# Sort-attention and gated MLP on one core: column sums of Sinkhorn by fp32 matmul, the first q as fp32, more transposes by DMA, the flag read in mid stream

## The chip, the cores and the metric

The kernel runs on one core of a Trainium2 chip. The metric is the device time of one execution in microseconds (us). The core has a matmul engine (TensorE, PE; its weight loads are listed apart as PEld), a vector engine (VectorE, DVE), an activation engine (ScalarE, ACT), GpSimd (POOL) and SyncE (SP). SP and POOL issue transfers to the DMA engines; SP's go by the hardware queue, POOL's by the software queue, which here also changes fp32 to bf16 on the way. Each engine takes its instructions in the order in which the program gives them.

## The reference

Inputs are fp32: q, k, v of shape (4, 8, 768, 64) (batch, head, sequence, head width), a sorting matrix of 8 x 8 for each batch and head, and the weights of a gated MLP. Cut to what matters:

```python
P = sort_net                                    # (4, 8, 8, 8)
for _ in range(5):
    P = P - np.max(P, axis=-1, keepdims=True)
    P = np.exp(P)
    P = P / (np.sum(P, axis=-1, keepdims=True) + 1e-09)
    P = P / (np.sum(P, axis=-2, keepdims=True) + 1e-09)
k_sorted = np.einsum('bhij,bhjcd->bhicd', P, k_b)   # 8 blocks of 96 rows are mixed
v_sorted = np.einsum('bhij,bhjcd->bhicd', P, v_b)
scores = scale * np.matmul(q_b, k_sb.transpose(0, 1, 2, 4, 3))  # inside a block, 96 x 96
attn = softmax(scores); x = attn @ v_sb             # (4, 768, 512) after merging heads
h = np.maximum(x @ w_in, 0.0); u, v = h[..., :512], h[..., 512:]
v_n = (v - mean(v)) / np.sqrt(var(v) + 1e-06)
v_s = np.einsum('ts,bsd->btd', w_spatial, v_n) + b_spatial[None, :, None]
out = (u * v_s) @ w_out                             # (4, 768, 512) fp32
```

## The kernel before

All of the work is cut into small units, functions named `u_XX`, and a text, `ORDER`, lists them in the order in which they are issued. An item such as `KT:2:D:0:2` calls `u_KT` with the arguments 2 (the PSUM tile), D (copied out by DVE; A is ACT), 0 (batch), 2 (pair of heads). The order in this text is the order on every engine: an engine that waits for one unit's data holds up all later units on it. There are four PSUM tiles, `ps0` to `ps3`, each used by one unit at a time.

The first part, for each batch: `L` loads q, k, v (POOL's queue, to bf16); `S0` loads the sorting matrices (SP's queue); `SK` is one Sinkhorn round, on 32 partitions (one for each batch and head) of 64 numbers: an exponential on ACT, then on DVE a row sum, a reciprocal, a product, a column sum, a reciprocal, a product. The maximum is left out; whether the sums stayed in range is looked at afterwards (`CK`, `CF`), and a flag is set for a slower general path if they did not. `PR` spreads the result over 128 partitions by matmuls, `P0` (DVE, batch 0) and `PD` (POOL, later batches) make of it block matrices `pd`, by which PE mixes k (`KT`, both mixed and turned) and v (`VT` and `VB` for batch 0; `VM` and eight SBUF-to-SBUF moves `VC` on SP's queue for the others). `QT` and `QQ` turn q on PE (one or two pairs of heads). `SC` makes the scores of four blocks and their exponential on ACT; `AT` multiplies by v and divides on DVE, giving `x_sb`. That has to be turned for the next product: `XT` does it on PE, with a copy from PSUM; `XD` does it by a DMA transpose on SP's queue.

The second part, for each batch: `VP` and `UP` are the two halves of the product with `w_in` (with relu on ACT or DVE), `ST`, `LN`, `LA` the normalization, `WT` the turning of `w_spatial` on PE (once), `SP` the spatial product and its bias on DVE, `GT` the gate, `OP` the product with `w_out`, `OE` its copy from PSUM and `OS` the transfer to the output. The second part of a batch is woven into the first part of the next. `OP` for the last batch is split: the first three of four inputs first, the fourth when it is ready. `o_sb` has two buffers, so a tile waits until the transfer of the tile two before it has landed.

`DM` are matmuls on zeros at the start, 36 in all, whose result is not used. `CK` (five checks on DVE), `CF` (a matmul that joins them, and two DVE steps that write the flag) and `LF` (every engine reads the flag into a register) stand at the end of `ORDER`; the branch follows. `BI` loads the bias over all partitions on SP's queue.

What sets the order around the change: POOL's queue holds, in this order, q, k and v of batch 0, v and k of batch 1, building `ident`, q of batch 1, then weights; SP's queue holds the sorting matrices, and nothing else until the first `VC`.

## Time and profile before

| | us |
|---|---|
| median of three runs (164.16 to 164.29) | 164.26 |
| the profiled execution: its own time | 163.99 |
| its span, from the first to the last instruction | 162.2 |
| PE, DVE, ACT, POOL busy | 147.9, 117.7, 84.3, 33.7 |
| mean granted clock of PE | 0.988 |

A page of the profile lists engines' busy times, groups of instructions by source line with the mean length of one, and the chain of work that ended last, followed back from the end. Lines such as `L569 PE MATMUL ps<-wspT,v_sb` name the source line, the engine, and what is written from what. The busy time in tenths over 40 slices of the span (about 4 us each) and the rates of the DMA engines:

```profile
PE   6988999899999979999999999999999999999700
DVE  4797899667897853748898888789787798267500
ACT  3144999858976476577654453557400155402420
DMA  2999999999999990479985996002059200243370
GB/s 12 191 204 205 203 205 205 210 220 237 271 206 204 206 172 0 69 133 148 184 188 94 225 149 195 0 36 97 0 107 237 113 0 0 91 172 129 129 250 25
```

The groups of instructions of the units in question, with busy time and mean length:

```profile
L307 PE MATMUL ps<-ident,q_in 128*64 128x128 bf16 x192 | 7.0, 220 | 1.1 <-DMA q_in<-in_q_dram 0.5 <-DVE kt L109 0.3 <-issue 0.3
L498 PE MATMUL ps<-ident,x_sb 96*128 96x96 bf16 x64 | 3.7, 206 | 0.0
L219 PE MATMUL ps<-warm 128*128 128x512 bf16 x35 | 9.9, 436 | 1.3 <-DVE warm L192 1.3
xT<-x_sb SPq DMA_TRANSPOSE x4, 5.1
```

(The last is from the list of transfers: four issued by SP, 5.1 us from issue to landing in the middle.)

### The profile page before, as it was taken

The numbers are of one execution on the slowest core, as the hardware profiler recorded it, in microseconds if no ns is written. First come the engines' busy times: TensorE is split into PE (matmuls) and PEld (weight loads), VectorE is DVE, ScalarE is ACT, GpSimd is POOL, SyncE is SP. The second block draws the span as 40 slices with busy tenths as digits, with TensorE's granted clock in tenths as the row PEclk, the third lists the DMA queues.
The fourth block names the chain that finished last, engine by engine and source line by source line (L and its number), as shares of the span: only waits on it lengthen the run. The fifth ranks groups of instructions, "written<-read, shape, count | busy, mean of one in ns | idle before, by whom it ended". The sixth has DMA issues, their size and how long they took to land.

```text
span 162.2 us, 3967 instructions
## 1 busy us (share of the span) xinstructions
PE 147.9 (91%) x1646; PEld 89.5 (55%) x1657; DVE 117.7 (73%) x265; ACT 84.3 (52%) x118; POOL 33.7 (21%) x39
## 2 busy tenths in 40 slices
PE   6988999899999979999999999999999999999700
PEld 2345777756677755455657656555666445655300
DVE  4797899667897853748898888789787798267500
ACT  3144999858976476577654453557400155402420
POOL 7946322470000434280000001600000000120000
PEclk9999999999999999999999999999999999999995
DMA  2999999999999990479985996002059200243370
GB/s 12 191 204 205 203 205 205 210 220 237 271 206 204 206 172 0 69 133 148 184 188 94 225 149 195 0 36 97 0 107 237 113 0 0 91 172 129 129 250 25
DMA packets 27351, 23.20 MB, mean 143 GB/s; under 512 B 7232, under 2 KB 24128, under 8 KB 27328
## 3 DMA queue, kind: packets, MB, share of 16 engines
q0 software_dynamic: 14864, 12.19, 48.5%
q1 hardware_dynamic: 12464, 10.70, 25.8%
q8 instruction: 14, 0.23, 0.5%
q14 instruction: 9, 0.07, 0.1%
HBM read 24.78 MB, written 6.29 MB: 192 GB/s over the span
## 4 chain that ended last, share of the span: by engine, by line
PE 78%; ACT 7%; DVE 6%; DMA 2%; issue 2%; DVEq 0%; ACTq 0%
PE ps L569 20%; PE ps L557 13%; PE ps L514 13%; PE ps L595 11%; PE ps L468 4%; PE ps L422 4%; PE ps L363 3%; PE ps L390 3%; PE ps L307 3%; ACT ex L427 2%; ACT kt L107 2%; PE ps L498 2%; DMA out_dram<-o_sb 1%; PE ps L504 1%; ACT o_sb L107 1%
## 5 line engine op out<-in xcount | busy, mean ns | idle before, releaser
L569 PE MATMUL ps<-wspT,v_sb 128*128 128x384 bf16 x192 | 33.2, 326 | 0.0
L427 ACT ACTIVATE ex<-ps 96x768 bf16<-96x768 f32 x32 | 24.4, 806 | 12.4 <-PE ps L422 12.3
L585 POOL TENSOR_TENSOR gt<-z,u_sb 128x768 bf16<-128x768 f32 x7 | 11.4, 1640 | 92.7 <-DVE z L575 42.1
L569 PEld LDWEIGHTS <-v_sb 128*128 128x128 bf16 x192 | 18.2, 98 | 11.9 <-issue 0.2
L575 DVE TENSOR_TENSOR z<-ps,b_bc 128x768 f32<-128x768 f32 x16 | 15.3, 957 | 11.6 <-PE ps L569 11.5
L557 PE MATMUL ps<-xT,w_in_sb 128*128 128x384 bf16 x128 | 23.3, 326 | 0.0
L476 DVE TENSOR_TENSOR x_sb<-ps,rec_all 96x512 bf16<-96x512 f32 x32 | 22.0, 687 | 1.1
L514 PE MATMUL ps<-w_in_sb,xT 128*128 128x512 bf16 x89 | 22.2, 379 | 0.4
L595 PE MATMUL ps<-w_out_sb,gt 128*128 128x512 bf16 x93 | 22.0, 379 | 0.2
L107 ACT COPY o_sb<-ps 128x1024 f32<-128x1024 f32 (+1 forms) x12 | 9.8, 835 | 14.8 <-PE ps L595 12.9
L531 DVE BATCH_NORM_STATS2 stats<-v_sb 128x6 f32<-128x512 bf16 x24 | 16.2, 677 | 1.0 <-ACT v_sb L113 0.9
L113 ACT ACTIVATE v_sb<-ps 128x1024 bf16<-128x1024 f32 (+1 forms) x8 | 7.4, 920 | 17.6 <-PE ps L514 17.6
L557 PEld LDWEIGHTS <-w_in_sb 128*128 128x128 bf16 x128 | 11.8, 98 | 7.6
L595 PEld LDWEIGHTS <-gt 128*128 128x128 bf16 x96 | 9.2, 98 | 10.2
L514 PEld LDWEIGHTS <-xT 128*128 128x128 bf16 x96 | 9.0, 98 | 9.6 <-DVE x_sb L476 0.2
L113 ACT ACTIVATE u_sb<-ps 128x768 bf16<-128x768 f32 x13 | 10.6, 812 | 5.1 <-PE ps L557 5.0
L107 ACT CAST kt<-ps 128x768 bf16<-128x768 f32 (+1 forms) x14 | 8.7, 641 | 7.9 <-PE ps L363 5.5
L468 PEld LDWEIGHTS <-ex 96*128 96x128 bf16 x256 | 10.5, 97 | 3.6 <-issue 0.3
L468 PE MATMUL ps<-vb,ex 96*128 96x65 bf16 x256 | 11.9, 193 | 0.1
L219 PE MATMUL ps<-warm 128*128 128x512 bf16 x35 | 9.9, 436 | 1.3 <-DVE warm L192 1.3
L422 PE MATMUL ps<-qT,kt 64*128 64x96 bf16 x256 | 9.5, 204 | 1.6 <-ACT kt L107 1.3
L422 PEld LDWEIGHTS <-kt 64*128 64x128 bf16 x256 | 6.2, 94 | 6.9 <-issue 3.8
(87 smaller groups left out, 179.0 us busy)
## 6 DMA issues: line engine op xcount, KB each, us to landing
out_dram<-o_sb SPq DMA_DIRECT2D x9, 512.0 KB, 4.3
q_in<-in_q_dram POOLq DMA_DIRECT2D x4, 768.0 KB, 18.0
k_in<-in_k_dram POOLq DMA_DIRECT2D x4, 768.0 KB, 15.1
v_in<-in_v_dram POOLq DMA_DIRECT2D x4, 768.0 KB, 21.5
vb<-vm SPq DMA_DIRECT2D x24, 99.0 KB, 3.1
out_dram<-o_sb SPq DMA_DIRECT2D x6, 256.0 KB, 3.2
ws_in<-in_moe_w_spatial_dram POOLq DMA_DIRECT2D x2, 576.0 KB, 26.4
w_in_sb<-in_moe_w_in_dram POOLq DMA_DIRECT2D x2, 512.0 KB, 26.0
```

Source lines behind the costliest of these rows:

```text
L107: nc.scalar.copy(out=out, in_=in_)
L113: nc.scalar.activation(out=out, in_=in_, func=AF.Relu)
L422: nc.tensor.matmul(t[:, hh, 0:HW].rearrange("p (g x) -> p g x", g=G)[:, :, ii * TB:(ii + 1) * TB], lhsT=kT[rows, i * BLK:i * BLK + 128], r ...
L427: nc.scalar.activation(out=e_tile(b, hp, ih).rearrange("p h (x g) -> p h x g", g=G), in_=t[0:BLK, :, 0:HW].rearrange("p h (g x) -> p h x g ...
L468: nc.tensor.matmul(t[:, hh, ii * VW:ii * VW + D + 1], lhsT=e[:, c:c + 128], rhs=vb[b % 2][:, ih * NI + ii, 2 * hp + hh, 0:D + 1], start=Tr ...
L476: nc.vector.tensor_mul(out=x_sb[:, hp].rearrange("p i (h d) -> p h i d", h=2), in0=tv[:, :, :, 0:D], in1=_raw_ap(rec, 0, [rec.ap[0], [NI, ...
L514: nc.tensor.matmul(t[:, x, :], lhsT=st["xT", b][:, n // 3, kc, (n % 3) * 128:(n % 3 + 1) * 128], rhs=w_in_sb[:, kc, DH:DFF], start=(kc == ...
L531: nc.vector.bn_stats(out=stats, in_=st["v_sb", b, n])
L557: nc.tensor.matmul(t[:, x, 0:HW], lhsT=w_in_sb[:, kc, mc * 128:(mc + 1) * 128], rhs=st["xT", b][:, ih, kc, :], start=(kc == 0), stop=(kc = ...
L569: nc.tensor.matmul(t[:, x, 0:HW], lhsT=st["v_sb", b, n][:, mc * 128:(mc + 1) * 128], rhs=wspT[:, 3 * x:3 * x + 3, n, :], start=(n == 0), s ...
L575: nc.vector.tensor_add(out=z.rearrange("p (x c) -> p x c", x=2), in0=t[:, :, 0:HW], in1=b_bc.rearrange("p (x c) -> p x c", x=2),)
L595: nc.tensor.matmul(t[:, x, :], lhsT=st["gt", b, mc][:, (n0 + x) * 128:(n0 + x + 1) * 128], rhs=w_out_sb[:, mc, :], start=(mc == 0), stop=( ...
```

## The change

Five things change together, and `ORDER` is written anew.

1. *Sinkhorn.* The sorting matrices lie as 2 halves of 128 rows (16 batch-and-head pairs of 8 rows each) of 8 numbers; a half is batches 0 and 1, or 2 and 3. `SX` does the exponential, with the row sum summed by the same ACT instruction, a reciprocal and a product by a per-row number on DVE. `SK` makes the column sums, already spread over the rows of their block, by one fp32 matmul with the matrix `same` (128 x 128, ones where two rows belong to one pair; built once by `SB` on DVE and POOL), then a reciprocal from PSUM and a product on DVE. In the first round ACT copies the column sums for the later check. In the last round the result is written as bf16 and spread 16 times along the row (`p_sp`); `PR` turns it by one matmul for each half. The mask is made by eight matmuls (`MK`) and not by a DVE sum.
2. *The first q.* `LH` loads q of batch 0 as fp32, in two halves, by SP's queue right after the sorting matrices; `QC` casts it to bf16, two pairs of heads on POOL and two on ACT. POOL's queue now first builds `ident` and `same`, and then loads k and v of batch 0 in halves, heads 4 to 7 before 0 to 3 for k. The mixing begins with heads 4 and 5.
3. *Transposes by DMA.* The output of batch 1's attention is turned by `XD` (it was `XT`). q of batch 3 is loaded early, put in order by four POOL copies (`QP`) and turned by one DMA transpose (`QX`); it was two `QQ`.
4. *The flag.* `CK` follows the last `AT` of batch 3, `CF` the next `OP`, and `LF` stands some ten units later, in the middle of the last batch's second part.
5. *Warm matmuls.* 10 `DM` matmuls in place of 36. A new unit `WX` is defined and not used.

The first and the last lines of the new `ORDER`, and the part with the turned output:

```diff
+ID BH S0:0 SB CO IV:2 S0:1 LH:0 SX:0:0 LH:1 L:k:0:4:8 SX:1:0 L:v:0:4:8 L:v:0:0:4 L:k:0:0:4 QC:P:0 L:v:1:0:8 L:k:1:0:8
+QC:P:3 IV:1 L:wv L:q:1:0:8 DM:0:4:512 SK:1:0:0 SX:0:1 MK:3 SK:3:1:0 IV:0 SK:0:0:1 SX:1:1 DM:0:1:512 L:wu SX:0:2
+DM:3:1:512 SK:2:1:1 QC:A:1 SK:3:0:2 SX:1:2 SX:0:3 QT:0:D:0:1 QC:A:2 DM:3:1:512 L:q:3:0:8 DM:2:1:512 SK:2:0:3 SK:3:1:2
+SX:0:4 QT:2:D:0:0 DM:1:2:512 SK:3:0:4 SX:1:3 L:wsa QT:3:A:0:3 PR:2:0 PC:A:0 P0:4:6 PD:1:0:4 P0:6:8 SK:1:1:3 SX:1:4
+VT:3:A:0:2 P0:2:4 PD:1:4:8 P0:0:2 QT:1:A:0:2 KT:0:A:0:2 SK:3:1:4 VB:2:D:0:2 VT:3:A:0:1 KT:1:D:0:3 SC:0:0:2:0
...
+AT:1:1:0:0 LA:0:5 SC:0:1:1:0 WT:3:A:0 LA:0:1 AT:1:1:3:0 AT:0:1:1:0 WT:2:A:4 XD:1:0 BI L:v:2:0:8 WT:3:D:2 LA:0:3
+SC:1:1:2:1 WT:0:D:3 WT:3:D:5 KT:1:D:2:1 KT:2:A:2:2 AT:0:1:2:1 KT:3:A:2:3 KT:2:A:2:0 AT:1:1:0:1 XD:1:1 SP:3:0:1
+VM:2:A:2:3 VM:1:D:2:0 L:q:2:0:8 SP:0:0:3 VM:2:D:2:2 VM:3:A:2:1 VC:2:0:4 GT:P:0:3 QQ:1:A:2:2 QQ:0:D:2:0 VC:2:4:8
+QX:3:0:4 VP:2:D:1:0:1 SC:1:2:3:1 SC:0:2:0:1 VP:3:A:1:4:5 SC:2:2:1:0 GT:D:0:1 ST:1:1 SC:1:2:2:1 L:v:3:0:8 ST:1:0 ST:1:4
...
+UP:2:A:3:1:1 GT:D:2:2 SP:1:3:0 SP:3:3:1 GT:P:3:0 SP:1:3:2 OP:3:2:4 GT:P:3:2 OS:1:4 OE:A:2:4 OS:1:0 OP:2:2:2 OP:1:2:0
+OE:A:2:0 GT:D:3:1 SP:0:3:3 GT:D:3:3 OS:2:4 OP:1:3:0:0:3 OS:2:0 OE:A:2:2 OP:0:3:2:0:3 OP:-1:3:0:3:4 OE:A:3:0:1:2
+OP:-1:3:2:3:4 OE:A:3:0:0:1 OP:2:3:4:0:3 OS:2:2 OE:A:3:2:1:2 OS:3:0:1:2 OP:-1:3:4:3:4 OE:A:3:2:0:1 OS:3:0:0:1
+OS:3:2:1:2 OS:3:2:0:1 OE:A:3:4:0:1 OE:A:3:4:1:2 OS:3:4:0:1 OS:3:4:1:2
```

The new functions, cut to the path taken:

```diff
+    def u_SB():
+        nc.vector.memset(same, 1.0)
+        for base, way in ((0, 1), (NB - 1, -1)):
+            nc.gpsimd.affine_select(
+                out=same, in_=same, compare_op=ALU.is_ge, fill=0.0, base=base,
+                pattern=[[-way * NB, 128 // NB], [0, NB]], channel_multiplier=way)
+    def u_SX(half, n, safe=False):
+        x, e, r = p_in[:, half], p_ex[:, half], p_row[:, half]
+        rows = (first_r if n == 0 else sums)[:, half]
...
+            nc.scalar.activation(out=e, in_=x, func=AF.Exp, accum_out=rows)
+        nc.vector.reciprocal(out=inv[:, half], in_=rows)
+        nc.vector.tensor_scalar(out=r, in0=e, scalar1=inv[:, half], scalar2=None, op0=ALU.mult)
+    def u_SK(ps, half, n, safe=False):
+        to = p16[:, half] if n == 4 else p_in[:, half]
+        t = ps_tile(ps)[:, 0, 0:NB]
+        nc.tensor.matmul(t, lhsT=same, rhs=r, start=True, stop=True)
...
+            if n == 0:
+                nc.scalar.copy(out=first_c[:, half], in_=t)
+            nc.vector.reciprocal(out=e, in_=t)
+        nc.vector.tensor_mul(out=to, in0=e, in1=r)
+        if n == 4:
+            nc.vector.tensor_copy(out=p_sp[:, half], in_=to.to_broadcast([128, NB, TB]))
+    def u_PR(ps, half):
+        t = ps_tile(ps)[:, 0, 0:128]
+        nc.tensor.matmul(t, lhsT=p_sp[:, half].rearrange("p j t -> p (j t)"), rhs=ident, start=True, stop=True)
+    def u_LH(half):
+        lo = int(half) * H // 2
+        st["q32", int(half)] = t = ld.tile([128, H // 2, G * D], FP32, name="q32", tag="ld")
+        nc.sync.dma_start(out=t, in_=_raw_ap(q, lo * S * D, [[G * D, 128], [S * D, H // 2], [1, G * D]]))
+    def u_QC(eng, hp):
+        to, of = st["q", 0][:, 2 * hp:2 * hp + 2], st["q32", hp // 2][:, 2 * (hp % 2):2 * (hp % 2) + 2]
+        if eng == "P":
+            nc.gpsimd.tensor_copy(out=to, in_=of)
+        else:
+            copy(eng, to, of)
```

`QP`, `QX` and `XD` are in the kernel before (`QP` and `QX` unused there).

More of the change, by code (lines that the diff above doesn't have):

```diff
@@ L650, in general_path @@
         st.clear()
[L651 to L656 removed]
+        for half in range(2):
+            u_S0(half)
+            for n in range(5):
+                u_SX(half, n, safe=True)
+                u_SK(0, half, n, safe=True)
+            u_PR(0, half)
+            if half == 0:
+                u_P0(0, 8)
+            u_PC("A", half)
         for b in range(B):
```

160 lines of the change are left out of this document (71 added, 89 removed).

## The prediction

> **What bounds the kernel now.** I read the page's engine totals first, then busy time by windows, then the chain of waits and the time line of the two ends, then the landing times of the transfers.
>
> ```profile
> span 162.2 us, 3967 instructions
> PE 147.9 (91%) x1646; PEld 89.5 (55%) x1657; DVE 117.7 (73%) x265; ACT 84.3 (52%) x118; POOL 33.7 (21%) x39
> PE 78%; ACT 7%; DVE 6%; DMA 2%; issue 2%; DVEq 0%; ACTq 0%
> ```
>
> The matmul engine sets the time, but not everywhere. The windows (length, then busy time of PE, PEld, DVE, ACT, POOL, granted clock, DMA share, GB/s) show two stretches where it is not full:
>
> ```profile
> 13.20:33.30 20.10, 18.27 (x415) 14.72 (x416) 16.28 (x32) 17.20 (x24) 7.93 (x10) 1.00 1.28 205
> 55.60:59.90 4.30, 3.43 (x90) 2.85 (x88) 2.44 (x4) 2.76 (x6) 1.64 (x1) 1.00 1.28 202
> ```
>
> From 13.2 to 33.3 us ACT and DVE, which empty PSUM, are busy 17.2 and 16.3 of 20.1 us: they pace the first batch's attention. The chain of waits through the second stretch (start, length, what) names the second batch's output, turned on PE (L498), and then the copies of `xT` and `kt`:
>
> ```profile
> 55.59 0.36 PE ps L498 x8
> 55.97 0.80 ACT xT L107
> 56.76 0.39 ACT kt L107
> 57.18 0.42 DVE kt L109
> 58.12 0.56 DVE kt L109
> 58.70 0.49 ACT kt L107
> 59.58 0.43 PE ps L390 x2
> ```
>
> At the start one Sinkhorn round is six steps one behind another. The last round's exponential starts at 9.43 us, the one before at 7.67, so a round takes 1.76:
>
> ```profile
> 9.43 0.26 ACT L231 ACTIVATE p_all<-p_all 32x64 f32<-32x64 f32 x1 [1.50 <-DVE p_all L242]
> 9.95 0.19 DVE L235 RECIPROCAL rowsum<-rowsum 32x8 f32<-32x8 f32 x1
> 10.18 0.21 DVE L236 TENSOR_TENSOR p_all<-p_all,rowsum 32x64 f32<-32x64 f32 x1
> 11.19 0.23 DVE L244 STREAM_TRANSPOSE p_t<-p 32x64 bf16<-32x64 bf16 x1
> ```
>
> At the end the last copy is done at 155.39 us, and SP then waits for the last output transfers to land; it passes the last of its landing waits at about 160.0. Its read of the flag lies under that wait:
>
> ```profile
> L639 SPq TENSOR_LOAD <-flag x1: 912/912/912, 156.2 to 156.2; - x1
> L696 SPq EVENT_SEMAPHORE  x8: 17/17/17, 157.7 to 160.0; - x8
> ```
>
> **The change, part by part.** The sum is made against the profiled execution: span 162.20, its time 163.99, so 1.79 us lie around the span; it is 0.27 below the median of 164.26, to which I add the difference.
>
> *Start, up to the first L514 matmul (32.84 us now).* Removed: five rounds on 32 rows of 64, `spread`, the stream transpose. Added: two interleaved halves of 128 rows of 8. Per round and half: exponential 0.26 (L231), reciprocal 0.19, multiply 0.21, fp32 matmul, reciprocal 0.19, multiply 0.21, and five hand-overs of 0.04 (9.95 to 10.18 for a 0.19 instruction). The fp32 column sum and an exponential that also sums are not in the trace. The nearest matmul is L634's, 128x5 at 0.17 us; from above I take four such matmuls (an fp32 number is two bf16 wide, a product four of theirs), each with a weight load of 0.10 (PEld rows), 1.1. I take 0.3, as the 8 columns are like the 5 of L634. A round is then 1.6, five 8.0. The first exponential can start at 2.4 as now (the table load ends at 2.03; the sort matrix landed 1.6 after its issue). To the 10.4 come: 0.3 for the copy of the first column sums on ACT, 2.0 because in PE's queue two `QT` of 12 transposes (at the slow pace shown below) and four warm matmuls (0.22 to 0.43 each) stand ahead of the column sums, and on DVE two 0.55 copies; 0.2 spread, 0.4 turn and 0.4 `P0` (0.415 at L263). Some 13.9; with 0.5 for the other half's steps in the same queues, the first mixing matmul starts at 14.4, where it is 13.17 now. Between 13 (all of the 2.0 hidden) and 15.5.
>
> From there ACT paces. Ahead of the first `VP` its new order has 21 copies or exponentials: 3 `VT`, 1 `QT`, 5 `KT`, 8 scores, 3 `VM`, 1 `XT`, each 0.78 to 0.81 (L107, L427), 16.9 in all. From 14.9 with 0.7 of idle (ACT is busy 9.6 of 10 us between 20 and 30) that is 32.5. DVE has 14.6 in the same stretch and hides. Term: **-0.3**, bounds -2.0 and +2.5.
>
> The first q goes by SP as fp32 (two transfers of 768 KB in SBUF), and POOL's queue starts with k and v halves instead. Now a 768 KB bf16 tensor lands every 3.8 us (q 7.5 us after its issue at 1.3, k 10.3 after 2.3, v 13.2 after 3.2), bound by the rate, so q, k and v are in by about 16.4 as before; but the halves used first land by about 12. The four casts of q cost about 0.8 on ACT (two) and up to 1.6 on POOL (two); ACT's lie in the gaps of its 1.5 us waits for DVE. If q were late there, the next exponential would be: nothing in the sum, inside the bounds.
>
> *PE work after the first `VP`.* By spacings in the chain (`VP` and `OP` 1.73 for 8 matmuls, `UP` 1.30, `SP` 1.95, `SC` 0.225, `AT` 0.24, `KT` 0.335, `VM` 0.325, `XT` 0.40, `WT` 0.335, `QQ` 0.67): 93.6 of second-part matmuls in both. Before: 23 `SC`, 24 `AT`, 8 `KT`, 8 `VM`, 4 `XT`, 6 `WT`, 4 `QQ`, 22.5. After: 24, 25, 8, 8, 2, 6, 4, 22.2. So 116.1 becomes 115.8: **-0.3**. (Over the whole kernel 1.3 of `QQ` and 1.6 of `XT` go; the new order reaches its first `VP` with that much less done.) PE needs 120.1 for its 116.1 now (32.84 to 152.97), 4.0 of holes.
>
> *The hole at 55.6.* Here 2.97 of PE work takes 4.3. The `XT` copies on ACT (0.80) leave, and eight units stand where `KT` alone stood. **-1.0**, between -1.4 and 0.
>
> *Second batch's output by DMA.* `XD:1:0` and `XD:1:1` go on SP's queue with the 384 KB bias load between them. Such a transpose takes 5.1 us on a quiet queue; the `vb` moves show what loads do to SP's transfers:
>
> ```profile
> DMA to landing us min/median/max: 7.1/7.9/8.2
> ...
> DMA to landing us min/median/max: 2.7/2.7/2.9
> ```
>
> (`vb` issued at 31 to 36 us beside loads, and at 66 to 70 alone.) Between the last `AT` of each half and its first reader stand 10.0 and 8.9 us of PE work, about 1 of it used by DVE. At 5.1 nothing waits; at 5.1 times 7.9/2.7, 14.9, PE would wait up to 7, but the loads of q, k and v of batch 2 end near 57 us, inside the wait. **+0.7**, between 0 and 3. POOL waits for q of batch 3 (landed near 37) before its first `QP`; behind it stand the loads of batch 2 and the `PD` products. k of batch 2 then lands near 49, its reader is at 52. By the Trainium skill, page "DMA: Bandwidth & Descriptors", section "Latency and other measured facts", DMA transposes move 261 GB/s; a 384 KB half would take 1.5 us by that, and the term would be 0; the trace's 5.1 (4.6 to 5.5) is over three times that, and I go by the trace.
>
> *Last q by DMA.* Four POOL copies (1.1 to 1.64 each, L275 and L585) and one 768 KB transpose, about 10 us of SP's queue; its reader stands 28 us of PE work later. Hidden; without that cover, up to 10.
>
> *Flag read early.* Each engine loads a register: 0.49 on PE's sequencer in mid stream, **+0.4** (0 to 0.5). Behind it wait `SP:1:2:3` on PE and the output of batch 1 on SP; DVE has the flag ready if it is less than 8 us behind PE (`CF` to `LF`). The five checks (about 1.7 of DVE) move ahead of `LA` of batch 2, which has some 8 us until it is read. At the end nothing is won by itself: SP's 0.91 and its branch lie under landings that end 2.3 us later.
>
> *End.* Now, counted from where the first tile of the last batch is summed (150.85), the copies of the last `o` tile wait for a landing at 154.17, and the last two issues (154.93, 155.79) land 4.2 and 4.0 later, behind two issued at 153.97 and 154.43. In the new order the middle tile is finished 6 matmuls (1.3) sooner and copied on ACT at once, so its transfers are issued about 1.5 us earlier and the last two have the queue alone: 2.2 to 2.5 each, as the pair at 151.47 and 151.95. **-1.3**, between -1.7 and +0.5 (the last tile of batch 2 lands late and holds a buffer).
>
> Sum: -0.3 -0.3 -1.0 +0.7 +0.4 -1.3 = -1.8: span 160.4, time 162.2, and on the median **162.5**.
>
> **The rivals.**
>
> *A, slower: the fp32 column sum is dear.* If each takes 1.1, five of them put the start back by 4.0: 166.5. Slower than before from 0.66 each (1.8 over five rounds). For it: no row shows a fp32 matmul. Against: the row of 0.17. By the Trainium skill, page "FP8 and Floating Point Precision", section "TensorE Precision Notes", true FP32 takes four passes through the array, which speaks for the upper end, but states no time.
>
> *B, the clock.* The warm matmuls of now start 0.43 apart until 4.68 us, then 0.22:
>
> ```profile
> 3.82 0.15 PEld L219 LDWEIGHTS <-warm 128*128 128x128 bf16 x1 [0.28 <-issue]
> 4.25 0.15 PEld L219 LDWEIGHTS <-warm 128*128 128x128 bf16 x1 [0.28 <-issue]
> 4.68 3.12 PEld L219 LDWEIGHTS <-warm 128*128 128x128 bf16 x15 [0.28 <-issue]
> ```
>
> So about 3.4 us of steady work come before the full pace. The new order has 10 warm matmuls for 36, and PE idles through the rounds. If the mixing matmuls start at half pace, 3.4 us yield 1.7: time 164.2, no change. Against: ACT, not PE, paces there. The rule is in the Trainium skill, page "TensorE: Matmul & The Clock Gate", section "What's actually happening": half rate by default and after about 3.4 us of idling; the spacings agree.
>
> *C, faster: the rounds hide.* If the half rounds take 1.5 and nothing in PE's queue delays them, the first mixing matmul starts near 12.4, when the first halves of k and v have landed: -2.0 more, 160.5.
>
> *D, slower: the transposes wait for the loads.* With the `XD` terms at 3, 164.8.
>
> **How the numbers follow.** Forecast 0.46, A 0.14, B 0.10, C 0.20, D 0.10. The likeliest gives 162.5, with its own range of 161.0 to 164.0. For 8 in 10 I go down to 160.0 (C) and up to 165.6 (D, and A half way). A difference of 0.2%, 0.33 us, is about what can be told from none. Faster: C, most of the forecast, a third of B, 0.68; the same: B and a little of the forecast, 0.08; slower: A, D and the rest, 0.24.
>
> **What would show it.** The first mixing matmul (`pd`, L393) near 14.4 and the first `VP` near 32.5; L251 matmuls near 0.3; no wait of `VP` of batch 1 on the DMA of `xT` over 1 us; the register load a gap of at most 0.5 on PE; the last output landing about 7.5 us after the first last-batch tile is summed, where it is 8.9 now. The forecast is wrong if the first `VP` starts after 34, if PE waits for k, v or `xT` of the middle batches, or if the last landing takes as long as now.

## The result: slower, by three waits in the middle and a later start

The changed kernel takes 170.85 us in the median of four runs (170.5 to 171.51), the kernel before 164.27 beside it (164.16 to 164.5): a ratio of 1.0403, 95% interval 1.0367 to 1.0439. The profiled execution has a span of 169.3 and a time of 171.07; before had 162.2 and 163.99. So the span grew by 7.1 us where the prediction had 1.8 less. Here and below a median counts every run, and a ratio leaves out those that lie more than 1.5% above the fastest of their kernel.

The engine totals of the page after:

```profile
span 169.3 us, 3851 instructions
PE 148.8 (88%) x1561; PEld 92.1 (54%) x1573; DVE 116.3 (69%) x266; ACT 83.6 (49%) x133; POOL 41.3 (24%) x49
PE 63%; DVE 15%; DMA 10%; ACT 3%; issue 3%; POOL 1%; SPq 0%; DVEq 0%; ACTq 0%
```

PE is as busy as before. The last line, the chain that ended last, says where the time went: transfers (DMA) hold 10% of it where they held 2%, and DVE 15% where it held 6%.

Busy time by windows of the kernel after (columns as before: length, then PE, PEld, DVE, ACT, POOL, granted clock, DMA share, GB/s):

```profile
16.80:34.40 17.60, 16.50 (x335) 13.76 (x335) 13.96 (x32) 15.54 (x24) 3.44 (x4) 1.00 1.30 205
34.40:47.90 13.50, 13.39 (x178) 8.27 (x177) 12.24 (x24) 7.76 (x11) 8.54 (x10) 1.00 1.21 227
47.90:57.50 9.60, 8.67 (x172) 6.73 (x169) 9.21 (x23) 7.84 (x13) 0.30 (x1) 1.00 1.42 185
57.50:67.30 9.80, 7.38 (x88) 4.73 (x84) 4.47 (x7) 3.22 (x5) 0.79 (x1) 1.00 0.71 117
72.00:79.50 7.50, 5.25 (x48) 3.14 (x48) 4.46 (x10) 2.62 (x4) 0.00 (x0) 1.00 1.23 222
79.50:161.60 82.10, 81.30 (x641) 45.48 (x647) 57.83 (x118) 36.16 (x50) 12.13 (x7) 1.00 0.48 113
```

The kernel before, at the places of the third window and of the last three (its window from 55.60 is in the prediction):

```profile
46.50:55.60 9.10, 9.10 (x135) 6.39 (x133) 7.54 (x18) 5.69 (x7) 1.64 (x1) 1.00 1.30 204
59.90:70.00 10.10, 10.05 (x82) 5.46 (x82) 5.64 (x8) 6.83 (x9) 3.80 (x3) 1.00 0.31 51
70.00:153.00 83.00, 82.56 (x704) 46.82 (x708) 65.53 (x128) 35.70 (x49) 7.18 (x6) 1.00 0.51 113
```

From 79.5 us on PE is as full as before (81.30 of 82.10); nearly all that is lost more lies ahead of that. In the window from 57.5 no engine is full and DMA is at 0.71: one particular transfer is waited for. In the window from 72.0 DMA is full at 222 GB/s: PE waits among loads. The chain of waits through both (start, length, what):

```profile
55.84 0.59 SPq L516
...
56.49 7.10 DMA b_bc<-in_moe_b_spatial_dram
...
64.55 0.96 DVE vm L111
...
72.57 6.53 DMA vb<-vm
79.10 0.04 issue
79.14 0.31 PE ps L498 x5
```

The first wait is for the bias `b_bc`. SP issues its load only behind the first DMA transpose (L516), it lands at 63.59, and the first addition of the bias on DVE has stood there for 5 us, with the PSUM copies of `vm` and all of PE behind it. The second is for the last of the eight moves of `vb`: issued at 72.57, landed 6.5 us later, where the moves of this batch took 2.7 before. DVE's waits, by what they wait for (us, times, longest), show the first from its side:

```profile
DVE z L612 <- DMA b_bc<-in_moe_b_spatial_dram: 5.0, 1, 5.0
```

To add it up I take from a trace the start of the first matmul of every unit of the second part; the time between two such starts, less the PE spacings of the matmuls issued between them (the prediction's spacings), is what that stretch loses.

| us | before | after | difference |
|---|---|---|---|
| first `VP` | 32.84 | 34.40 | +1.6 |
| PE work from there to the end | 116.0 | 115.7 | -0.3 |
| lost up to the first `SP` (47.9 to 57.5 after) | 0.3 | 2.8 | +2.5 |
| lost at the stretch of 55.6 before | 1.3 | 0 | -1.3 |
| lost at the bias | 0 | 3.2 | +3.2 |
| lost at the moves of `vb` | 0.2 | 2.8 | +2.6 |
| all other losses | 2.3 | 2.7 | +0.4 |
| last PE work to the end of the span | 9.2 | 7.7 | -1.5 |
| span | 162.2 | 169.3 | +7.1 |

(The rounded differences add up to 7.2.) The first row is that of one execution. The seven profiled kernels that keep the changed start, this one and six below, have the first mixing matmul at 16.6 to 16.9 and the first `VP` anywhere from 34.4 to 36.6, so +1.6 is near the least that the new start costs.

### The profile page after: what moved, and what is told of

It is laid out like the page before. It is cut to its first block, busy times and chain, and to the rows that moved or that the text cites. A ratio compares the mean times of both kernels' runs of the same rounds, so it can differ in the third digit from the quotient of the medians.

```text
span 169.3 us, 3851 instructions
## 1 busy us (share of the span) xinstructions
PE 148.8 (88%) x1561; PEld 92.1 (54%) x1573; DVE 116.3 (69%) x266; ACT 83.6 (49%) x133; POOL 41.3 (24%) x49
## 3 DMA queue, kind: packets, MB, share of 16 engines
q1 hardware_dynamic: 20000, 13.85, 33.5%
## 4 chain that ended last, share of the span: by engine, by line
PE 63%; DVE 15%; DMA 10%; ACT 3%; issue 3%; POOL 1%; SPq 0%; DVEq 0%; ACTq 0%
PE ps L551 12%; PE ps L632 11%; PE ps L594 10%; PE ps L606 10%; DMA b_bc<-in_moe_b_spatial_dram 4%; DMA vb<-vm 4%; PE ps L393 4%; PE ps L452 3%; DVE x_sb L506 3%; PE ps L322 3%; PE ps L498 3%; DVE z L612 2%; PE ps L251 2%; DVE v_sb L580 2%; DMA out_dram<-o_sb 2%
## 5 line engine op out<-in xcount | busy, mean ns | idle before, releaser
L622 POOL TENSOR_TENSOR gt<-z,u_sb 128x768 bf16<-128x768 f32 x8 | 13.8, 1721 | 87.7 <-DVE z L612 46.9
L109 ACT COPY o_sb<-ps 128x1024 f32<-128x1024 f32 (+1 forms) x13 | 10.1, 819 | 17.5 <-PE ps L632 15.5
L498 PE MATMUL ps<-vb,ex 96*128 96x65 bf16 x256 | 12.7, 193 | 2.6 <-DMA vb<-vm 2.2
L115 ACT ACTIVATE u_sb<-ps 128x768 bf16<-128x768 f32 x12 | 9.7, 810 | 7.5 <-PE ps L594 7.3
L115 ACT ACTIVATE v_sb<-ps 128x1024 bf16<-128x1024 f32 (+1 forms) x9 | 8.4, 928 | 8.5 <-PE ps L551 8.4
L505 DVE RECIPROCAL rec_all<-ps 96x8 f32<-96x8 f32 x32 | 6.3, 198 | 8.7 <-PE ps L498 8.4
L109 ACT CAST vm<-ps 128x768 bf16<-128x768 f32 x9 | 7.2, 797 | 6.1 <-PE ps L420 6.1
L622 DVE TENSOR_TENSOR gt<-z,u_sb 128x768 bf16<-128x768 f32 x8 | 7.6, 947 | 3.6 <-PE ps L632 3.5
## 6 DMA issues: line engine op xcount, KB each, us to landing
k_in<-in_k_dram POOLq DMA_DIRECT2D x3, 768.0 KB, 16.6
```

The lines of the kernel that those rows point to most:

```text
L109: nc.scalar.copy(out=out, in_=in_)
L115: nc.scalar.activation(out=out, in_=in_, func=AF.Relu)
L498: nc.tensor.matmul(t[:, hh, ii * VW:ii * VW + D + 1], lhsT=e[:, c:c + 128], rhs=vb[b % 2][:, ih * NI + ii, 2 * hp + hh, 0:D + 1], start=Tr ...
L622: eng.tensor_mul(out=gt, in0=st["z", b, mc], in1=st["u", b, mc // 2][:, mc % 2])
```

## The experiments

Eighteen kernels ran, each beside the kernel before. Edits are shown as the items of `ORDER` that move. Each result gives the median in us, then the ratio to the kernel before and its 95% interval; what was lost where is read from one profiled execution, in us. Names with a are the changed kernel with an edit, names with b the kernel before with one part of the change.

### The bias, the moves and the start, one at a time

**a_bias**: the bias load ahead of the first DMA transpose.

```diff
- VC:1:0:4 SC:2:1:2:0 ... XD:1:0 BI L:v:2:0:8
+ VC:1:0:4 BI SC:2:1:2:0 ... XD:1:0 L:v:2:0:8
```

> The changed kernel with the bias load moved ahead of the first DMA transpose in SyncE's queue (behind the first batch of moves to vb), nothing else. Theory 1 (the wait at 57 to 65 us is the bias load's: it is issued at 56.5 behind the transpose, lands at 63.6, and the first addition of the bias, whose PSUM tile the next matmuls need, waits for it): the stretch from 55.8 to 67.3 us loses its 3.8 us of holes, time 166.5 to 168. Theory 2 (the transposes beside the loads are the wait, and the bias only covers it; they land at 62.7 and 64.9): the products that read xT wait in its place, at least 2 of the 3.8 us stay, time 169 to 171.

169.61 us, ratio 1.0307 (1.0264 to 1.0351). The bias lands at 47.4 and the 3.2 at its place becomes 0.4, so that cause stands. But 1.2 was won, not 2.8: the first `VP` of this execution was 0.9 later, and the moves of `vb`, which now begin 2 us sooner, still end beside the loads and cost 3.9 for 2.8; the end is 0.4 shorter. The windows show a second price of such a hole:

```profile
72.00:74.40 2.40, 0.66 (x9) 0.37 (x7) 1.00 (x2) 0.00 (x0) 0.00 (x0) 0.95 1.24 235
74.40:77.80 3.40, 3.40 (x12) 1.51 (x10) 0.85 (x2) 0.00 (x0) 0.00 (x0) 0.54 1.26 225
77.80:79.00 1.20, 1.14 (x19) 0.75 (x20) 1.04 (x2) 0.70 (x1) 0.00 (x0) 1.00 1.27 190
```

PE does 0.66 of work in 2.4 us, and then its granted clock is half for 3.4 us: 12 matmuls fill them, 1.6 us lost on top of the wait.

**a_bias_loads**: a_bias, with v of batch 3 loaded right behind q of batch 2, and k of batch 3 and the last weight loaded behind the moves, because POOL now makes a later gate product ahead of them.

```diff
- VC:2:0:4 GT:P:0:3 ... L:v:3:0:8 ST:1:0 ... GT:D:0:2 ... L:k:3:0:8 ... L:wo
+ L:q:2:0:8 L:v:3:0:8 ... VC:2:0:4 GT:D:0:3 ... GT:P:0:2 ... L:k:3:0:8 ... L:wo
```

> As the run with the early bias load, and GpSimd's loads are rearranged: v of batch 3 is loaded right behind q of batch 2, k of batch 3 and w_out only after the second gate product of batch 0 (which GpSimd now does in place of the first), so that no load runs beside the moves to vb of batch 2. Theory 1 (the wait at 73 to 79 us is those moves beside the loads issued at 68 to 70): the moves land in 3 us each, the 3.2 us of holes go, time 163.5 to 165.5. Theory 2 (the moves are late in themselves, being queued late, or the earlier load of v makes the transposes of batch 1 later): 0 to 1 us against the run with the early bias load.

167.37, ratio 1.0175 (1.015 to 1.0201), the lowest median of the edited changed kernels, not to be told from that of a_qq_start below. The moves land 2.8 to 3.8 us after their issue and cost 0.2. But the first DMA transpose now meets the load of v, and PE waits for it. Its chain of waits:

```profile
54.38 12.08 DMA xT<-x_sb
66.46 0.04 issue
66.50 0.39 PE ps L551
```

v landed at 65.94, the transpose at 66.46: 2.3 lost there.

**a_qcact**: all four casts of the first q on ACT.

```diff
- QC:P:0 ... QC:P:3 ... QC:A:1 ... QC:A:2 ...
+ QC:A:1 ... QC:A:0 ... QC:A:3 ... QC:A:2
```

> The changed kernel with all four casts of the first q on ScalarE, none on GpSimd. Theory 1 (VectorE's small steps that take 0.7 to 0.8 us in place of 0.2 are held by a GpSimd cast that runs at the same time: two of them, 0.6 each): no such step is over 0.3 us, the first mixing matmul starts 1 to 1.5 us earlier (15.3 to 15.8 in place of 16.8), time 169.5 to 170.2. Theory 2 (the long steps have another cause, or the two more casts on ScalarE, 0.8 each, hold the exponentials as long): the start stays within 0.4 us.

170.45, ratio 1.0357 (1.0339 to 1.0376): no gain that can be told. The first mixing matmul came 1.05 sooner (15.73), as expected, yet the first `VP` 1.8 later (36.2). The later stage meets the later transfers otherwise: the bias, landed at 62.4, costs only 0.4, though its place in the queue is unchanged, and the moves cost 4.2. By shape, the matmuls of one head's mixing of v (12, busy us, mean ns) in the two kernels a_qcact and a_all (below), first turn each:

```profile
L393 PE MATMUL ps<-pd,v_in 128*64 128x128 bf16 x12 | 0.9, 310 | 0.9 <-DVE pd L277 0.9
```

```profile
L393 PE MATMUL ps<-pd,v_in 128*64 128x128 bf16 x12 | 0.5, 223 | 0.0
```

The same 12 matmuls take 0.9 in the one and 0.5 in the other: PE works at half pace, in a_qcact until 24.8 us, in the changed kernel until 20.2, in before only until 4.7. Whether the casts on ACT bring the longer half pace is open: a_qplate below has it until 25.5 with the start unchanged, and needs 19.9 from the first mixing matmul to the first `VP`, where a_qcact needs 20.5 and the changed kernel 17.6.

**a_warm**: 23 warm matmuls instead of 10 (the expectation miscounts them as 21).

```diff
- DM:0:1 ... DM:3:1 ... DM:3:1 ... DM:2:1 ... DM:1:2 ... SK:1:1:3
+ DM:0:3 ... DM:3:3 ... DM:3:3 ... DM:2:2 ... DM:1:4 ... SK:1:1:3 DM:0:4
```

> The changed kernel with 21 matmuls on zeros in place of 10, in the gaps of TensorE during the Sinkhorn rounds and one group of four just ahead of the first mixing matmul. Theory 1 (TensorE runs at half pace until 20.2 us, where spacings halve, for want of steady work): full pace at the first mixing matmul or within 1 us of it, first matmul of the second part up to 1 us earlier, time 170 to 170.8. Theory 2 (the copies from PSUM pace the stage, so the clock costs nothing; or the added matmuls stand ahead of the column sums and delay them): the first matmul of the second part within 0.3 us, or up to 1.5 us later.

171.18, ratio 1.0417 (1.0394 to 1.044): the time of the changed kernel. PE was at full pace from 9.7 us on and the first `VP` came at 33.5, 0.9 sooner, but the waits behind it grow: 3.3 lost at the bias and 3.4 at the moves, for 3.2 and 2.8. The four kernels with 22 or 23 warm matmuls (this one, a_all, a_qq_start, a_qq_wt) all need 17.0 from the first mixing matmul to the first `VP`; those with 10 need 17.6 to 20.5.

### Parts of the change alone, and two other cures

**b_tail**: the order of the last batch's tiles alone, in the kernel before.

```diff
- OP:0:3:4:0:3 ... OP:3:3:2:0:3 ... OP:-1:3:2:3:4 OE:D:3:2:1:2 ... OP:-1:3:4:3:4
+ OP:0:3:2:0:3 ... OP:-1:3:2:3:4 ... OP:3:3:4:0:3 OE:A:3:2:1:2 ... OP:-1:3:4:3:4
```

> The kernel before with the last batch's output tiles in the changed order alone (tiles 0, 2, 4, the middle one finished and copied at once), flag read last as before. Theory (the end is a gain of its own, independent of the rest): last PE work to end of span 7.7 where before has 9.2, so 162.7 to 163.0 in the median and nothing else moves. Rival (the tail is shorter in the changed kernel because the early flag read takes the waits at the end away): 9.2 stays, 164.3.

163.44, ratio 0.9957 (0.9944 to 0.9971), a gain of 0.7. From the last PE work to the end it takes 8.6, not 7.7.

**b_flag**: checks, flag and its read in mid stream.

```diff
- OP:3:3:2:0:3 CK OS:2:4 ... OS:3:4:1:2 CF:2 LF
+ GT:D:2:1 OE:A:1:4 CK SP:0:2:0 ... VP:1:A:3:0:1 CF:2 ... LF OP:2:2:0
```

> The kernel before with the five checks, the flag and its read moved into the last batch's first matmuls and the tail left alone. Theory (the register load is off the path, as it left no gap on PE in the changed kernel, and the end waits for the landings): 164.2 to 164.4, no change. Rival 1, my prediction's term: a gap of 0.4 to 0.5 on PE, 164.7. Rival 2: 0.5 to 1 is won at the end, 163.5.

164.83, ratio 1.0033 (1.0019 to 1.0047). Rival 2 was right about the end, which wins 0.8 (8.4 for 9.2). PE loses 1.5 at one place and 0.4 in small ones, 0.2 of it at the flag's matmul and nothing at the register load. The 1.5 comes from my place for the checks. The chain of waits of b_flag:

```profile
120.67 0.87 DVE gt L585
121.53 0.35 DVE ends L620
...
123.15 0.04 DVE bad L621
123.18 0.04 issue
123.23 0.97 DVE z L575
124.20 0.04 issue
124.24 2.11 PE ps L569 x12
```

Ten short DVE steps, 1.65 us, stand between a product and the bias addition `z` that empties PSUM for PE. In the changed kernel the checks stand where nothing is lost.

**a_qplate**: POOL's four copies for the last q behind the loads of batch 2.

```diff
- QP:P:3:2 L:k:2:0:8 QP:P:3:0 ... QP:P:3:3 ... QP:P:3:1 ... L:v:2:0:8 ... L:q:2:0:8
+ L:k:2:0:8 L:v:2:0:8 ... L:q:2:0:8 QP:P:3:0 QP:P:3:1 QP:P:3:2 QP:P:3:3
```

> The changed kernel with POOL's four copies for the last q behind the loads of k, v and q of batch 2 instead of ahead of them. Theory (POOL's first copy waits for q of batch 3 until 39.4 us, and k, v and q of batch 2 are loaded behind it at 40 to 47; so the bias, the transposes and the moves of vb meet these loads): the loads are issued 6 to 15 us sooner and land by about 52, the bias lands within 5 of its issue and its hole falls from 3.2 to under 1.5; 168.5 to 169.5. Rival 1 (the transfers are late because the rate of all transfers is used up until 60 us whatever their order): bias hole stays over 2.5, 170.5 to 171. Rival 2 (the copies of the last q then meet the next batch's products): a new wait, over 171.

169.74, ratio 1.0322 (1.0273 to 1.0371); the profiled execution, 172.0, is the longest of its four. q of batch 2 was issued at 38.6 for 47.3 and landed at 57.7 for 59.8: nine us of earlier issue are worth two, because the loads run back to back. The bias cost 0.9 (its load still follows the transpose, but took 5.5); but this execution's first `VP` came at 36.6, 2.2 later, and a_qcact, also late, has the small bias wait with POOL's copies in place, so the 0.9 can't be put down to this edit. The first rival is mostly right: what counts is how many bytes stand in the queue, not when POOL asks.

**a_noxd**: the second batch's output turned on PE again.

```diff
- XD:1:0 BI ... XD:1:1
+ XT:2:A:1:0:0 XT:3:D:1:0:2 BI ... XT:1:A:1:1:0 XT:2:D:1:1:2
```

> The changed kernel with the second batch's output turned by 16 PE transposes and four copies, as before, in place of the two DMA transposes; the bias load then follows the moves of vb on SP at once. Theory (the transposes themselves are not waited for, but the bias load queued behind the first is): the bias is issued at about 38 and lands before 48, the bias hole goes (-3), PE works 1.6 more, and ACT and DVE get four copies of 0.4 to 0.8 in a stretch where they already pace (+0.5 to 1.5): 170 to 171, about that of the changed kernel and above the bias moved alone (169.6). Rival (the DMA transposes delay the loads and the moves of vb as well): the second hole, 2.2 + 0.6, shrinks too, and the time is 168 or less.

175.31, ratio 1.0646 (1.0559 to 1.0732): worse than either theory. The bias hole goes (0.4), but the stretch from 47.9 loses 5.3 for 2.8, PE works 1.6 more, and the moves, 2 us later, cost 5.2, 1.8 of it at half clock. In the changed order the four copies find no room, so turning by DMA is the cheaper way there; its price is the bias load behind it on SP's queue.

### Is a DMA transpose late because of loads?

**b_xd**: the two DMA transposes alone, in the kernel before.

```diff
- XT:1:A:1:0:2 ... XT:0:D:1:1:2 XT:3:A:1:0:0 ... XT:2:A:1:1:0 ... VP:3:D:1:0:1 VM:2:A:2:0 SP:1:0:0
+ AT:3:1:1:0 XD:1:0 ... AT:2:1:1:1 XD:1:1 ... VM:2:A:2:0 SP:1:0:0 VP:3:D:1:0:1
```

> The kernel before with the second batch's output turned by two DMA transposes instead of 16 PE transposes and four copies, the bias load where it was (ahead of them), and the first tile of the batch's hidden product one unit later to give the second transpose time. PE works 1.6 less. Theory (a transpose is hidden when no load and no bias stands beside or behind it): both land about 5 us after issue, the wait at the first tile is under 1, the hole at 55.6 (1.3) shrinks: 162.3 to 163.3. Rival (the loads of batch 2 and of v of batch 3 end only near 57 here too, so the transposes take 9 to 12): a wait of 2 to 4 takes the gain: 164.3 to 166.

167.98, ratio 1.0205 (1.0171 to 1.024), against the theory. **b_xd3**: the same, with the loads of v of batch 3 and of the last weight behind the transposes.

```diff
- L:wo ... L:v:3:0:8 ... GT:P:0:2
+ GT:P:0:2 L:v:3:0:8 L:wo
```

> b_xd with the loads of v of batch 3 and of the last weight behind the two DMA transposes instead of ahead of them. Theory (a DMA transpose lands only when the loads issued before it have landed: 64.7 beside 64.4 there): the transposes land within 6 us of their issue, by 57 and 62, and neither is waited for over 0.5; 162.0 to 163.5, under before. Rival (the transpose takes 10 us or more whenever SP issues it in mid kernel): the wait stays, 166 or more.

167.43, ratio 1.0159 (1.0104 to 1.0213). What writes `xT` in b_xd and then in b_xd3 (duration of the issue on SP, and below it the time to landing, both in min/median/max):

```profile
L486 SPq DMA_TRANSPOSE xT<-x_sb x6: 1320/1610/7330, 51.0 to 125.9; - x6
...
DMA to landing us min/median/max: 3.8/4.8/13.7
```

```profile
L486 SPq DMA_TRANSPOSE xT<-x_sb x6: 1310/1486/2752, 50.8 to 125.5; - x6
...
DMA to landing us min/median/max: 3.8/4.2/5.6
```

The theory of the cause holds: 13.7 with loads ahead of the transpose (it landed at 64.66, the load of v issued 16 us before it at 64.44), 5.6 and 4.3 with them behind. Its time does not: neither kernel waited for the `xT` of this batch, since I had moved the first reader back. In their profiled executions, the longest of each kernel (170.4 and 169.6, where the others have 167.3 to 168.4 and 166.0 to 167.8), both lost 3.7 to 3.9 at the moves of `vb` instead; how much of that the other runs lost is not shown. In b_xd POOL issues the load of k at 69.00 us, and the last move, issued at 69.53, lands 6.6 later; in before that move goes out at 70.33, 0.14 ahead of the load, and lands 2.9 later. In b_xd another 2.4 or so went into short waits of the new order from 46 to 70 us.

### The rest together

**a_late**: a_bias, with one product of the first batch on POOL instead of DVE ahead of the loads, to hold them back.

```diff
- GT:D:0:1 ST:1:1 ... L:v:3:0:8
+ GT:P:0:1 ST:1:1 ... L:v:3:0:8
```

> The changed kernel with the bias load ahead of the first DMA transpose and one product of the first batch on POOL instead of DVE, so that the loads of v and k of batch 3 and of the last weight start about 1.7 us later and the moves of vb of batch 2 run before them. Theory (the second hole is these moves beside these loads): the moves land 3 us after issue but for the last, the second hole falls from 2.2 + 1.8 (bias moved alone) to under 1.5, no new wait for the transposes since nothing is loaded beside them: 166.5 to 168. Rival (v of batch 3 then comes late for its mixing, or the holes only move): 169 or more.

170.55, ratio 1.0389 (1.0355 to 1.0424). It missed its aim: the loads were issued from 67.5 on, the moves until 70.6, and the last four moves landed 5.7 to 7.0 after issue. There 4.4 were lost, 1.4 of it at half clock.

**a_all**: a_late with the casts on ACT and the 23 warm matmuls of a_warm.

> a_late with the four casts of the first q on ACT and 11 more warm matmuls. Theory (the start is late by DVE's steps held beside POOL and by PE at half pace; once the later waits for transfers are gone its gain reaches the end): first VP at 32.5 to 33.5, 164.5 to 166.5, within 1.5% of before. Rival (a transfer that comes at a fixed time takes the gain again, as it did with either of the two alone): the first VP comes sooner and the time is that of a_late.

169.99, ratio 1.0285 (1.0208 to 1.0361); four runs from 168.1 to 171.3, too wide to tell from a_late. The first `VP` came at 33.9, and 5.1 were lost at the moves for 4.4 in a_late, so it went as the rival had it.

**a_qq**: the last q turned on PE as before and loaded late; v of batch 3 in its place in the row of loads; the bias early; k of batch 3 and the weight behind the moves.

```diff
- L:q:3:0:8 DM:2:1:512 ... QP:P:3:2 L:k:2:0:8 QP:P:3:0 ... QX:3:0:4 ... L:wo ... OE:A:0:4 ... OE:A:0:2
+ L:k:2:0:8 L:v:2:0:8 L:q:2:0:8 ... BI ... L:v:3:0:8 ... L:wo L:q:3:0:8 ... OE:A:0:4 QQ:1:A:3:0 ... OE:A:0:2 QQ:3:D:3:2
```

> The changed kernel with the last q turned on PE as before (its load late, in place of the early one), so that k, v and q of batch 2 are loaded as soon as their buffers are free and v of batch 3 follows them at once; k of batch 3 and the last weight only behind the moves of vb; the bias ahead of the first DMA transpose. Theory (the early load of the last q takes 3.8 us of a stretch in which the loads run back to back, and what no longer fits there, v of batch 3 and the last weight, comes beside the moves of vb): loads are done by about 58, both transposes land within 5 us, the two holes (3.2 and 2.8 in the changed kernel) are under 0.5 each, PE works 1.3 more: 166.0 to 167.5. Rival (the transfers of SP are slow for their own sake): a hole of over 2 stays at one of the two places, over 168.5.

168.02, ratio 1.0227 (1.0197 to 1.0258). Its windows, at the same times as those of after:

```profile
47.90:57.50 9.60, 8.68 (x161) 6.62 (x161) 9.17 (x24) 7.48 (x13) 0.00 (x0) 1.00 1.33 206
57.50:67.30 9.80, 9.75 (x124) 6.12 (x123) 7.29 (x10) 4.51 (x6) 0.00 (x0) 1.00 0.60 92
67.30:72.00 4.70, 4.70 (x46) 2.62 (x47) 4.31 (x9) 3.79 (x5) 0.00 (x0) 1.00 0.81 138
72.00:79.50 7.50, 7.44 (x63) 4.31 (x62) 6.39 (x14) 3.94 (x5) 4.17 (x4) 1.00 0.58 75
```

PE is full where it had 7.38 of 9.8 and 5.25 of 7.5: both holes are gone (0.4 and 0.2), the transposes land 5.5 and 3.6 after issue. That is the theory; the time is half a us over its range. The first `VP` was at 35.0 here, 0.6 later than in the changed kernel's profile; that PE works 1.4 more was in the range.

**a_qq_start**: a_qq with the casts on ACT and 12 more warm matmuls.

> a_qq with the four casts of the first q on ACT and 11 more warm matmuls. Theory (with the waits for transfers gone the start's 1 to 2 us reach the end): first VP at 32.5 to 33.5, 1 to 2 under a_qq, near before's 164.3. Rival (as in the three runs before, a transfer at a fixed time takes it): the time of a_qq.

167.53, ratio 1.0194 (1.0165 to 1.0222), 0.5 under a_qq with intervals that overlap. PE ends its work 1.55 sooner than in a_qq (157.05 for 158.60), with the first `VP` 1.6 sooner: with no transfer waited for, the start does reach PE's end. But the end took 8.3 for 7.4 in the profiled execution, so half was given back there.

**a_qq_wt**: in a_qq_start, the first three weight-transpose units 6 to 10 us earlier, and all six copies on ACT.

```diff
- UP:1:A:0:0:0 WT:3:A:1 ... WT:3:A:0 ... WT:2:A:4 ... WT:3:D:2 ... WT:0:D:3 WT:3:D:5
+ UP:1:A:0:1:1 WT:2:A:2 ... UP:1:A:0:1:0 WT:3:A:1 ... UP:1:A:0:0:0 WT:3:A:0 ... WT:2:A:4 ... WT:0:A:3 WT:3:A:5
```

> a_qq_start with the first three weight-transpose units moved 6 to 10 us forward into room on ACT and the other copies of that kind on ACT instead of DVE. Theory (what is left beside the start is the stretch from 47 to 57 us, 2.8 over its PE work, where DVE is busy 9.1 of 9.5 because the weights that these units turn were loaded 4 to 9 us later than before): the hole falls to 1.5 or less, 166 to 166.7. Rival (the exponentials and the scores set this stretch, not DVE): the hole stays, 167.5.

170.14, ratio 1.0346 (1.0312 to 1.038). The theory falls: the hole became 4.6, with 3.4 us at half clock in it, and 1.2 came ahead of it. A copy of `wspT` takes 0.80 on ACT and 0.54 on DVE; both engines are near full there (after: DVE 9.2, ACT 7.8 of 9.6). That the stretch is paced by what ACT and DVE have to empty together fits this and a_noxd; which of it is late is not settled.

### The end, and the best version

**b_all** is b_xd with both steps of the end, **b_end** only the end's two steps, the checks behind the last normalization, and **b_best** is b_end with the transposes and held loads of b_xd3 and the first reader of `xT` at its old place.

The flag in b_all:

```diff
- VP:0:D:3:2:3 GT:D:2:2 ... OE:A:2:0 LA:3:4 SP:1:3:2 SP:3:3:0 ... OS:3:4:1:2 CF:2 LF
+ VP:0:D:3:2:3 CK GT:D:2:2 ... OE:A:2:0 CF:2 LA:3:4 SP:1:3:2 SP:3:3:0 LF
```

The flag in b_end and b_best:

```diff
- LA:3:4 SP:1:3:2 SP:3:3:0 ... SP:3:3:3 ... OS:3:4:1:2 CF:2 LF
+ LA:3:4 CK SP:1:3:2 SP:3:3:0 CF:2 ... SP:3:3:3 LF
```

> b_xd with the changed order of the last batch's tiles and the early flag read, the checks standing where DVE has room (behind the first hidden product of the last batch). Theory (the end's gain of 1.5 is 0.7 from the tiles and 0.8 from the flag, and adds to b_xd): 1.3 to 1.6 under b_xd; the last PE work to the end of the span 7.5 to 7.9. Rival (the early checks cost DVE what the end wins): 0.6 to 0.8 under b_xd.

> The kernel before with both of the end's steps, the checks behind the last batch's normalisation, where DVE waits for the next sums anyway. Theory (the two gains at the end, 0.6 and 0.8, add, and the 1.5 to 2 lost in b_flag and b_all were DVE's checks ahead of work that PE waits for): 162.6 to 163.1. Rival (the register load of PE or the fp32 sum of the flag costs PE): 163.2 to 163.8.

> The kernel before with b_xd3's two DMA transposes and held loads, the first hidden product of that batch back at its old place (so that the loads of k and q of batch 3 do not start while the last move of vb is still to be issued, as in b_xd3: 69.53 to 76.25), and both steps of the end (b_end). Theory (the transposes are worth PE's 1.6 where neither loads nor moves meet them): 161.5 to 162.7. Rival (the order around them, planned with copies, loses what PE wins): 163.5 or more, b_end stays the best.

b_all: 167.07, ratio 1.0176 (1.0144 to 1.0209), 0.9 under b_xd. Its end takes 7.3, but the checks ahead of the last normalization cost PE 2.4, as the rival had it. b_end: 163.95, ratio 0.9978 (0.9956 to 1.0). Of its ten runs two took 162.35 and 162.65 and eight 163.7 to 164.4; the profiled one is the first, with 7.5 at the end and no more than 0.4 lost on PE. Why the eight are over 1 us longer is open. b_best: its seven runs fall into two groups, 162.6 to 162.9 (three) and 167.6 to 168.8 (four); the ratio of the first is 0.9915 (0.9893 to 0.9937), the profiled execution, 168.7, is of the second. There the load of k was issued at 70.06 and the last move of `vb` at 70.48, and PE lost 5.1 to it and 1.6 more at half clock. The windows of b_best around it:

```profile
74.50:79.40 4.90, 0.05 (x3) 0.04 (x2) 0.00 (x0) 1.59 (x3) 0.00 (x0) 1.00 1.22 169
79.80:83.20 3.40, 3.40 (x19) 1.76 (x18) 1.67 (x4) 1.42 (x3) 0.00 (x0) 0.52 1.18 255
```

That the first group has the two the other way round fits, but no profile of it was taken. Reliably faster than both kernels is only b_tail, by 0.4%.

The end of five kernels, counted from the last PE work (us):

| | before | b_tail | b_flag | b_end | after |
|---|---|---|---|---|---|
| to the last output's issue | 2.8 | 2.9 | 2.8 | 2.8 | 3.1 |
| from there to its landing | 4.0 | 3.3 | 3.2 | 2.3 | 2.2 |
| landing to the end of the span | 2.4 | 2.4 | 2.4 | 2.4 | 2.4 |

In these profiles either step takes 0.7 to 0.8 off the landing of the last transfer, both take 1.7, and little else changes. For a single step that is one profile each. Both steps stand in fifteen profiled kernels: thirteen have 2.2 to 2.4 from the last issue to its landing, but a_qq_start and a_qq_wt have 3.2, so the two steps are not all that counts. Why a late flag goes with a longer landing the runs do not show.

## Why the prediction was wrong, point by point

| term | predicted | measured |
|---|---|---|
| first `VP` | -0.3 | +1.6 |
| PE work behind it | -0.3 | -0.3 |
| the hole at 55.6 | -1.0 | -1.3, and 2.5 new ahead of it |
| second batch's output by DMA | +0.7 | +3.2 |
| last q by DMA | 0 | +2.6 |
| flag | +0.4 | 0 at the register load, 0.2 at its matmul |
| end | -1.3 | -1.5 |

Two steps failed in the main: the wait that the second batch's output brings, and the cost of the last q, put at nothing.

**Second batch's output.** The step that failed: "the 384 KB bias load between them" was named as a transfer on SP's queue, and its reader was not looked up. The transposes themselves, on which the working spent its care, were not waited for (they landed at 62.7 and 64.9). The load behind the first was: it is the operand of the first addition on DVE. a_bias shows it, 3.2 to 0.4 (a_noxd too, where no transpose stands ahead of it). In before it was issued at 38.4 and landed at 45.8, ahead of the first addition (51.98); a step put ahead of a queued load moves that load.

**Last q by DMA.** The transpose was hidden, as predicted (landed 91.8). What was not priced is its load. The loads run back to back up to 60 us in both kernels; before has w_out (57.3) and v of batch 3 (61.2) in at the end of this stretch, the changed kernel has the q of the last batch (39.3) in their place, and brings v, k and the weight at 68 to 70, beside the eight moves. a_bias_loads and a_qq, which keep these loads away from the moves, each bring the 2.8 to 0.2. That these loads stand beside the moves because the early q took their place fits a_qq, which changes other things too, and stays argued. The working counted what the transpose asks of SP's queue, and not what its load asks of the rate.

**Start.** The first mixing matmul was put at 14.4, between 13 and 15.5, and came at 16.78. (The parts as listed add up to 13.7, not 13.9, and with the other half's 0.5 to 14.2; that is small beside the 2.4.) A half's rounds, by its exponentials, took 2.2, 2.7, 2.9 and 2.0, not 1.6. The fp32 column sum is two matmul records, 0.57 together, where 0.3 was put and 1.1 in rival A: its direction, a third of the way. In the first half DVE goes on 0.7 to 0.8 after the operand of the sum was ready in rounds two to four, and 1.1 after it in the last, behind a warm matmul at half pace, where 0.38 was put. And DVE is held by POOL. Four stretches of the time line of after:

```profile
3.35 0.57 PE L251 MATMUL ps<-p_row,same 128*128 128x8 f32 x2
...
6.37 0.82 POOL L363 CAST q_in<-q 128x768 bf16<-128x768 f32 x1 [0.94 <-DMA q<-in_q_dram]
6.40 0.81 DVE L259 TENSOR_TENSOR p_in<-p_ex,p_row 128x8 f32<-128x8 f32 x1
...
9.31 0.82 POOL L363 CAST q_in<-q 128x768 bf16<-128x768 f32 x1 [0.40 <-DMA q<-in_q_dram]
9.35 0.80 DVE L259 TENSOR_TENSOR p_in<-p_ex,p_row 128x8 f32<-128x8 f32 x1
...
12.00 0.17 DVE L259 TENSOR_TENSOR p_in<-p_ex,p_row 128x8 f32<-128x8 f32 x1
```

The same instruction takes 0.17 alone and 0.80 beside a cast on POOL. The casts were priced as "up to 1.6 on POOL", with ACT as the one who could be late; a_qcact, without them, has the mixing at 15.73, 1.05 of the 2.4. From there to the first `VP` it took 17.6 (18.1 predicted), so ACT's count was about right. Rival B was given 0.10 because "ACT, not PE, paces there": PE at half pace does cost there (20.5 in a_qcact, 17.0 in a_qq_start at full pace), so about 0.6 of the changed kernel's 17.6, and 2.8 of a_qplate's 19.9.

**Hole at 55.6.** It is gone, as predicted, but its new neighbour was not looked at: from 47.9 to 57.5 ACT and DVE pace PE. `w_spatial` landed at 42.9 and 45.9 there (34.2 and 41.3 before), so the six copies of `wspT` fall into it; a_qq_wt, which moved them, did not cure it, so this stays argued.

**Flag and end.** The sum, -0.9, was near the -1.5 by luck, out of two errors: the register load leaves no gap on PE (the flag's matmul costs it 0.2, in b_flag and in the changed kernel), and the early read does win 0.8 at the end of b_flag's profile, where the prediction had "nothing is won by itself". The tile order, given all of -1.3, is worth 0.7.

The range reached to 165.6 because each wait was bounded by itself; that two loads whose readers were not followed would each cost about 3 was in no rival. D came nearest, in the right place and for the wrong transfer. Of the prediction's signs of being wrong one came, the first `VP` after 34; PE waited for no k, v or `xT` of the middle batches, so the signs were blind to both large waits.

## What to carry to other kernels

For every load that a change moves past something in a queue, or that it adds, look up its first reader and the transfers that it will run beside, also when the step itself is hidden. Where loads run back to back, a transfer made earlier is another made later by the same bytes; ask which. A gain ahead of a wait for a transfer was worth nothing here until that wait was gone (a_warm against a_qq_start), so cure the waits first and measure the start last.

## What of the hardware was not expected

- A hole can cost twice. In ten of the profiled kernels the granted clock was 0.50 for about 3.4 us right behind a hole, some 1.3 to 2 us more, after 1.7 us of idle PE within 2.4 (a_bias), or 1.4 in pieces within 3.4 (a_qq_wt). The changed kernel's profile has holes as large and no half clock behind them, so what decides is open. The Trainium skill, page "TensorE: Matmul & The Clock Gate", section "What's actually happening", gives half rate after one idle window of about 3.4 us; the length of the half rate agrees, the idle time needed was less here.
- The granted clock reads 1.00 from 16.8 us on in after, while 12 matmuls take 0.9 there (mean 309 ns) that take 0.5 in a_all (223 ns): at the start half pace shows only in the lengths.
- A DMA transpose of `xT` landed only after the loads issued before it: 13.7 us in b_xd and 12.1 in a_bias_loads, within 0.6 of the load's own landing, and 3.8 to 5.6 in b_xd3, where the load of v goes behind it. A move of `vb` does not wait so: in after one issued at 68.76 lands at 75.11, the load of v issued before it, at 68.11, at 79.86. And SP stands at the issue of a transpose for up to 12 us (the last q's in after), with all that is queued behind it.
- Small DVE steps of 0.17 to 0.23 us take 0.5 to 0.8 while POOL casts 768 columns or issues a load (after, 3 to 10 us). The Trainium skill, page "GPSIMD Engine Reference", section "1. Specifications", has POOL share its SBUF interface with DVE when DVE has two SBUF inputs; the product at L259 has two and agrees. L244, with one such input and a number per row, takes 0.49 and 0.68 for 0.23 beside POOL's issue of a load.
- A move of `vb` that went out 0.14 us ahead of a 768 KB load landed in 2.9 us (before), one that went out 0.4 behind it in 6.9 (b_best).
